# Attention, a two-dimensional Fourier transform and a feed-forward block on one core: transforms folded further along the token axis, three transpose tiles, one set of scheduling preferences

## The chip, the core and the metric

The kernel runs on one core of one Trainium2 chip. The metric is the device time of one launch in microseconds (us), all four batches included. The engines are named as in the profile: PE (TensorE, matrix products), PEld (its weight loads), DVE (VectorE), ACT (ScalarE), POOL (GpSimd) and SP (the engine whose queue issues most of the transfers).

## The reference, cut to what matters

```python
# attention: 4 batches, 8 heads, 1152 keys, 64 features; pairs of queries are averaged -> 576 tokens
q_pool = q.reshape(B, H, S // 2, 2, D).mean(axis=3)
scores = scale * np.matmul(q_pool, k.transpose(0, 1, 3, 2))
attn = np.exp(scores - max) ; attn = attn / sum
attn_out = np.matmul(attn, v)                    # -> x: (4, 576 tokens, 512 channels)
# then per batch
X = np.fft.fft(np.fft.fft(x, axis=1), axis=2)    # over tokens and over channels
u = x + np.real(X)
un = (u - mean) / np.sqrt(var + 1e-06)
out = u + np.maximum(un @ w_ch1, 0.0) @ w_ch2    # 512 -> 2048 -> 512
```

## The kernel before, in words

**Order.** The kernel is written through a recording layer (`Model`). It keeps an estimated clock for every engine and for every operand, and the function `loop` picks at each step what PE gets next by these estimates: a piece of scores (`s_go`), transposes (`t_go`), a piece of weighted values (`a_go`), or a block of the feed-forward part (`block`, "f"). Small background work (loads, normalisations, the transform's elementwise steps) is fed in between by `poll` when an engine is estimated to have room. So the numbers in `_pe`, `_elementwise` and `mood` set the order of the instructions on each engine; the chip then runs each engine's list in order. `mood` draws, for each stretch of 40 us of estimated PE time, a set of preferences from a seed in the list `SEEDS`; `USUAL` is the set without a seed.

**Attention.** 16 pairs of heads, five units each: four units with both heads (128 queries each) and one half unit. A unit is: scores (18 products `s`, three key pieces of 384 columns; a unit of the first kind runs two heads in two row halves of the array), their scaled eviction with running minimum on DVE (`evict`), exp on ACT (`s_exp`), 36 transposes `t` of 64x64 (18 in a half unit) into two PSUM banks at a time, copies of these to SBUF (`pt` for eight key chunks, `ptc` for the ninth) on DVE or ACT, whichever is estimated to end first, and 18 products `o` with the values (`av`). PSUM has seven banks for all of `s`, `t` and `f`, and one for `o`. The tiles `pt` come from a ring of two, or are borrowed from the feed-forward part's rings `g` and `wraw`.

**Transform.** When the four pairs of a batch are done, `dft(b)` computes the real part of the two-dimensional transform. Channels are folded by symmetry into sums and differences (tiles `xs`), tokens too (token t with 576-t), so 289 of 576 token rows are left. The first products go over channels: for three chunks of token rows (97, 96, 96) the folded data are the weights, the tables `cc1` and `cs1` the moving side, split by frequency class (65, 64 and 128 columns for the cosine part, 128 and 128 for the sine part). ACT copies each result to `y`. The second products go over tokens: for two (sine) or three (cosine) column blocks, three products each with 289 moving columns of `cc2` or `cs2` accumulate in one bank; DVE adds the banks to `x` (16 adds over 128 partitions, and two over one). Then `norm(b)` does the layer norm with small products (`lsum`, `sq`, `dg`).

**Feed-forward.** Three fp32r products stand for one (`mm3`). Batches 0 to 2 give 512 of their 576 tokens, 512 columns a product; batch 3 takes the rest with its own, in 384 columns. These products (`f<-unh,w`, `f<-unl,w`, `f<-g,w`) fill gaps in the attention from batch 0's norm on, and are all that is left at the end.

Of the kernel before, what the change touches and what calls it, by code (L numbers as in the profile page):

```python
# [32 lines left out]
TOK = np.concatenate([np.arange(NH), np.arange(SQ - 1, HT, -1)])  # L33
# [12 lines left out]
TCH = [(0, 97), (97, 96), (193, 96)]  # L46
# [178 lines left out]
def _pe(m, op, out, ins, kw):  # L225
# [92 lines left out]
def fused_kernel(ctx: ExitStack, tc: tile.TileContext, k2, q2, v2, w1, w2, cst, out):  # L318
# [26 lines left out]
    cc2 = cp.tile([97, 3, NH], F32, name="cc2")  # L345
    cs2 = cp.tile([97, 3, NH], F32, name="cs2")
# [105 lines left out]
    def s_piece(pr, j, pc, after=None):  # L452
# [8 lines left out]
        for p, k in zip(ps, tiles):  # L461
            if pc == 0:
                sp[k] = spp.tile([P, S], F32, tag="sp", name="sp")
                bia[k] = smp.tile([P, 3], F32, tag="bia", name="bia", bufs=6)
# [25 lines left out]
    HOME = {"pt": (ptp, 2), "g": (gp, 4), "wraw": (cvp, 4)}  # L490
# [101 lines left out]
    def loop(units):  # L592
# [3 lines left out]
        home, where, exps = {}, {}, deque()  # L596
# [11 lines left out]
        def s_cand():  # L608
# [11 lines left out]
            r = [nc.slot("ps_t", "t", 7, len(unit_tiles(pr, j)))]  # L620
# [20 lines left out]
        def t_cand():  # L641
# [4 lines left out]
            if x == 0:  # L646
# [6 lines left out]
                if at["a"][0] < (i if ready and lag[0] or home.get(i - 1) == home[i] else i - 1):  # L653
                    return None
            tiles = unit_tiles(pr, j)
            ks = [tiles[x]] if x < len(tiles) else tiles
            t = nc.slot("ps_t", "t", 7, 2)
            for k in ks:
                if k in exps:
                    t = max(t, max(nc.t["act"], nc.ready(sp[k][:, :])) + 1280 * (exps.index(k) + 1))  # L660
                else:
                    t = max(t, nc.ready(sp[k][:, :]))
            return t

        def t_go():
# [3 lines left out]
            if x == 0:  # L669
                where[i] = {}  # L670
                if j == 0:
                    for x_, (t, r) in enumerate(((cc1, P), (cs1, P), (cc2, 97), (cs2, 97)) if pr == 1 else ()):
# [7 lines left out]
            ks = [tiles[x]] if x < len(tiles) else tiles  # L680
            while any(k in exps for k in ks):
                s_exp(*exps.popleft())
            if x < len(tiles):
# [17 lines left out]
        def a_cand():  # L701
            i, part = at["a"]
            if i == n or i >= at["t"][0]:
                return None
            w = where[i]
            t = 0.0
            for c in range(part * 3, part * 3 + 3):
                for y in range(2):
                    pt, o = w[y, c]
                    t = max(t, nc.ready(pt[:, :, o:o + D]))  # L710
# [55 lines left out]
    def dft(b):  # L766
# [6 lines left out]
        z = tmp[:1, 0, :NH]  # L773
# [18 lines left out]
        bs = mtile([P, NH], F32, "bs")  # L792
# [3 lines left out]

        sets = {0: [], 1: []}
        for y in (1, 0):
            for j in range(2):
                t = xs[y][:, j]  # L800
                yield SB, lambda e: ENG[e].tensor_tensor(t[:, 1:HT], t[:, 1:HT], t[:, NH:], op=(ALU.add, ALU.subtract)[y])
        for y in (1, 0):
            t = xs[y]
            a, c, o = t[:, 0, :NH], t[:, 1, :NH], (xs[1][:, 1, :NH], bs)[y]
            yield SB, lambda e: ENG[e].tensor_tensor(o, a, c, op=ALU.subtract)
            if y:
                yield SB, lambda e: ENG[e].tensor_tensor(a, a, c, op=ALU.add)
                yield CC, lambda e: copy(e, a[:1], c[:1])
                sets[1] += [(a, SSETS[0], slice(0, P)), (o, SSETS[1], slice(P, 2 * P))]
            else:  # L810
                yield SB, lambda e: ENG[e].tensor_tensor(c, a, c, op=ALU.add)
                yield CC, lambda e: copy(e, a, c)
                yield CC, lambda e: copy(e, c[:1], o[:1])
                yield CC, lambda e: copy(e, o[:1], z)
                sets[0] += [(a, CSETS[0], slice(0, 65)), (c, CSETS[1], slice(65, 129)), (o, CSETS[2], slice(129, 257))]

        parts = []
        for y, n in ((1, 256), (0, 257)):
            yy = mtile([97, 3, n], F32, f"y{y}")

            def first(t, t0, m):
                ps = bank()
                c = slice(t0, t0 + m)
# [4 lines left out]
            for t, (t0, m) in enumerate(TCH):  # L828
# [554 lines left out]
```

## Time and profile before

| what | value |
|---|---|
| median of 3 runs | 900.22 us (899.06 to 900.27) |
| the profiled execution | 899.82 us, of which the span of the program's instructions is 898.0 us |
| busy share of the span | PE 98%, PE's weight loads 84%, DVE 66%, ACT 52%, POOL 33% |
| granted TensorE clock, mean | 0.998 of full |

Busy times are from one profiled execution. PE's matmuls are pipelined, so a record's duration holds latency that overlaps its neighbours; what a product costs in a stream is the distance from its start to the start of the next. A product of two fp32 operands shows as two records in the trace and as one in the order of instructions.

### The profile page before, as it was taken

To read this page: it belongs to the slowest core of one execution; us is meant where nothing else is said; L and a number is where in the kernel's file an instruction comes from. 1 tells how busy PE (TensorE), PEld (TensorE's weight loads), DVE (VectorE), ACT (ScalarE), POOL (GpSimd) and SP (SyncE) were. 2 spreads that over 40 slices of the span, in tenths; PEclk is the share of its full clock that TensorE was granted. 3 is DMA by queue.
4 is the path that set the end of the run, shared out by engine and by line. 5 is a ranking of instruction groups with operands and counts; after the bars stand their busy time and mean duration, and the time that the engine had idled before them with its cause. 6 is when DMAs were issued, how large, how long until landed. Compare 5 with 4: busy or idle time off the path is not lost.

```text
span 898.0 us, 22733 instructions
## 1 busy us (share of the span) xinstructions
PE 878.6 (98%) x9044; PEld 755.3 (84%) x9044; DVE 591.0 (66%) x1608; ACT 464.7 (52%) x948; POOL 294.4 (33%) x386
## 2 busy tenths in 40 slices
PE   8999999999999999999998999999999999999998
PEld 6888888788888778878876888888877888999998
DVE  7888889898778978878867756444558323222222
ACT  5777899597667657957743655453522311110110
POOL 2334557655745765367543220300020000000000
PEclk9999999999999999999999999999999999999999
DMA  5553564156868482757570534423393667444432
GB/s 164 176 162 127 174 213 171 49 170 208 285 235 287 144 296 107 266 209 281 160 269 24 202 108 153 147 75 113 90 345 93 184 193 254 148 120 139 118 95 70
DMA packets 54686, 153.28 MB, mean 171 GB/s; under 512 B 15202, under 2 KB 18290, under 8 KB 54580
## 3 DMA queue, kind: packets, MB, share of 16 engines
q1 hardware_dynamic: 49972, 142.07, 47.6%
q0 software_dynamic: 2160, 8.85, 3.2%
q8 instruction: 71, 1.16, 0.5%
q10 hardware_dynamic: 2448, 0.92, 0.4%
q14 instruction: 35, 0.29, 0.1%
HBM read 129.06 MB, written 22.75 MB: 169 GB/s over the span
## 4 chain that ended last, share of the span: by engine, by line
PE 80%; DVE 8%; ACT 5%; issue 4%; DMA 1%; POOL 1%; DVEq 0%; ACTq 0%; POOLq 0%; SPq 0%
PE f L193 47%; PE o L193 14%; PE s L193 13%; PE t L193 7%; DVE sp L193 3%; ACT sp L193 1%; DVE xs L193 1%; ACT pt L193 1%; DVE wa L193 1%; DMA w<-w 1%; DVE pt L193 1%; ACT x L193 1%; DVE x L193 1%; DVE tmp L193 1%; DMA w<-wraw 0%
## 5 line engine op out<-in xcount | busy, mean ns | idle before, releaser
L193 PE MATMUL f<-g,w 128*128 128x512 f32 (+1 forms) x960 | 206.3, 371 | 2.5 <-DMA w<-w 1.3
L193 PEld LDWEIGHTS f<-g,w 128*128 128x128 f32 x960 | 173.2, 188 | 27.8 <-issue 1.9
L193 ACT ACTIVATE sp<-sp,bia 128x1152 f32<-128x1152 f32 x144 | 180.2, 1256 | 27.4 <-DVE sp L193 27.1
L193 PE MATMUL f<-unh,w 128*128 128x512 f32 (+1 forms) x640 | 186.2, 372 | 0.0
L193 DVE TENSOR_SCALAR_CACHE_REDUCE sp<-s,bia 128x384 f32<-128x384 f32 x288 | 162.8, 613 | 6.0 <-PE s L193 2.5
L193 ACT ACTIVATE g<-f 128x512 fp32r<-128x512 f32 (+1 forms) x80 | 44.3, 554 | 222.5 <-PE f L193 222.5
L193 PE MATMUL o<-pt,vs 128*64 128x128 f32 (+1 forms) x2560 | 145.8, 266 | 0.5 <-DVE pt L193 0.4
L193 PEld LDWEIGHTS o<-pt,vs 128*64 128x64 f32 x2560 | 126.9, 137 | 16.9 <-issue 11.7
L193 PEld LDWEIGHTS f<-unh,w 128*128 128x128 f32 x640 | 117.1, 188 | 16.4 <-issue 1.9
L193 DVE SCALAR_TENSOR_TENSOR g<-f,g 128x512 fp32r<-128x512 f32 (+1 forms) x80 | 50.8, 635 | 110.9 <-ACT g L193 110.7
L193 PE MATMUL s<-ksh,qh 64*128 64x384 f32 (+1 forms) x432 | 117.4, 389 | 4.7 <-ACT pt L193 1.1
L193 DVE TENSOR_TENSOR x<-f,x 128x512 f32<-128x512 f32 (+1 forms) x80 | 47.8, 597 | 107.3 <-PE f L193 107.2
L193 PE MATMUL f<-unl,w 128*128 128x512 f32 (+1 forms) x320 | 118.0, 369 | 0.0
L193 PEld LDWEIGHTS t<-ident,sp 64*128 64x128 f32 x2592 | 96.6, 138 | 23.1 <-issue 9.0
L193 PE MATMUL t<-ident,sp 64*128 64x64 f32 x2592 | 110.3, 226 | 4.7 <-DVE sp L193 2.6
L193 ACT COPY pt<-t 128x512 f32<-128x512 f32 x153 | 83.2, 588 | 54.6 <-PE t L193 54.0
L193 DVE COPY pt<-t 128x512 f32<-128x512 f32 x135 | 87.5, 684 | 29.7 <-PE t L193 29.0
L193 PE MATMUL s<-ksh,ql 64*128 64x384 f32 (+1 forms) x432 | 102.9, 350 | 0.1
L193 PE MATMUL s<-ksl,qh 64*128 64x384 f32 (+1 forms) x432 | 98.2, 339 | 0.0
L193 PEld LDWEIGHTS s<-ksh,qh 64*128 64x128 f32 (+1 forms) x432 | 62.7, 189 | 26.0 <-issue 4.4
L193 DVE TENSOR_SCALAR_CACHE_REDUCE sp<-s 128x384 f32<-128x384 f32 x144 | 74.8, 552 | 13.5 <-PE s L193 12.1
L193 POOL TENSOR_TENSOR wa<-wa,wk 128x256 int32<-128x256 int32 x64 | 46.1, 741 | 93.5 <-DVE wa L193 60.9
(100 smaller groups left out, 1038.7 us busy)
## 6 DMA issues: line engine op xcount, KB each, us to landing
w<-w SPq DMA_DIRECT2D x128, 512.0 KB, 3.5
wraw<-in_w SPq DMA_DIRECT2D x32, 512.0 KB, 4.1
w<-wraw SPq DMA_DIRECT2D x32, 512.0 KB, 3.7
qr<-in_q SPq DMA_DIRECT2D x15, 640.0 KB
vs<-in_v SPq DMA_DIRECT2D x16, 576.0 KB, 7.2
ksh<-in_k POOLq DMA_DIRECT2D x15, 576.0 KB, 5.5
kr<-in_k SPq DMA_DIRECT2D x15, 576.0 KB, 6.0
out<-x SPq DMA_DIRECT2D x12, 256.0 KB, 3.4
```

What stands on the lines that cost most here:

```text
L193: return real(*args, **kw)
```

## The change

1. **Transform.** Tokens are folded twice more: the 289 rows are ordered anew (`TOK`), sums and differences of rows t and 288-t are made, and of those with even frequencies once more. The first products then have four chunks of 71 to 76 token rows in place of three of 96 or 97, with the same moving columns. Each second product needs only the frequencies of its class: four products with 73, 72, 144 and 144 moving columns in place of three with 289. Their results are written to every fourth or every second column of the bank. The folds are new elementwise steps on DVE, POOL or ACT, some 14 a batch, between the old ones and the first products.
2. **Transposes.** The ring of `pt` has three tiles. When both heads' exps are near, a group of transposes takes four key chunks of both heads, not eight of one; the weighted values of a unit may start as soon as the chunks of their piece are there.
3. **Estimates and preferences.** The estimated price of fp32 products changes, the seeds are dropped (`SEEDS = []`, so `USUAL` holds throughout), and three new entries (`ws`, `wa`, `both`) tell how much of what follows is asked to be ready.
4. **Small.** The ring `bia` has five tiles (six before), `vt` one (two before). At the end, the second half of each output block of the last batch is sent from ACT's queue, not from SP's.

```diff
-TOK = np.concatenate([np.arange(NH), np.arange(SQ - 1, HT, -1)])
+QT, ET = HT // 2, HT // 4
+TOK = np.concatenate([np.arange(ET + 1), np.arange(QT - 1, ET, -1), [QT]])
+TOK = np.concatenate([TOK, HT - TOK[1:QT], [HT]])
+TOK = np.concatenate([TOK, SQ - TOK[1:HT]])
-TCH = [(0, 97), (97, 96), (193, 96)]
+CCH = [slice(0, 76), slice(71, 147), slice(147, 219), slice(219, 291)]
+SCH = [slice(0, 71), slice(71, 143), slice(143, 215), slice(215, 287)]
+OCH = [slice(0, NH, 4), slice(2, NH, 4), slice(1, NH, 2), slice(1, NH, 2)]
+KCH = [slice(0, 73), slice(73, 145), slice(145, 289), slice(289, 433)]
-        kind, cost = "M", max(n * 4 / 2.4, 112)
+        kind, cost = "M", max(n * 4 / 2.4 + 6, 155)
-    HOME = {"pt": (ptp, 2), "g": (gp, 4), "wraw": (cvp, 4)}
+    HOME = {"pt": (ptp, 3), "g": (gp, 4), "wraw": (cvp, 4)}
...
+            if x < len(tiles) and both[i]:
+                pt = t_tile(512, home[i])
+                spend(t_step(pt, [(k, 4 * x + c) for k in tiles for c in range(4)]))
...
+        a, c = slice(1, QT), slice(QT + 1, HT)
+        yield tt(fs[:, :, 143:286], es[:, :, a], es[:, :, c], ALU.add)
+        for i in (slice(0, 2), slice(2, 3)):
+            yield tt(fc[:, i, 148:291], ec[:, i, a], ec[:, i, c], ALU.subtract)
+        yield tt(es[:, :, a], es[:, :, a], es[:, :, c], ALU.subtract)
+        for i in (slice(0, 2), slice(2, 3)):
+            yield tt(ec[:, i, a], ec[:, i, a], ec[:, i, c], ALU.add)
+        yield tt(fc[:, :, 147:148], ec[:, :, 0:1], ec[:, :, HT:NH], ALU.subtract)
+        a, c = slice(1, ET), slice(ET + 1, QT)
+        yield tt(fs[:, :, :71], es[:, :, a], es[:, :, c], ALU.subtract)
+        yield tt(fs[:, :, 71:142], es[:, :, a], es[:, :, c], ALU.add)
+        yield CC, lambda e: copy(e, fs[:, :, 142:287:QT], es[:, :, ET:QT + 1:ET])
+        yield tt(fc[:, :, :71], ec[:, :, a], ec[:, :, c], ALU.add)
+        yield tt(fc[:, :, 76:147], ec[:, :, a], ec[:, :, c], ALU.subtract)
+        yield CC, lambda e: copy(e, fc[:, :, 71:76], ec[:, :, 0:NH:ET])
...
-                for t, (t0, kk) in enumerate(TCH):
-                    nc.tensor.matmul(ps[:m, :NH], lhsT=yy[:kk, t, j * P:j * P + m], rhs=c2[:kk, t, :],
-                                     start=t == 0, stop=t == 2)
+                for t, (c, o, k) in enumerate(zip(ch, OCH, KCH)):
+                    kk = c.stop - c.start
+                    nc.tensor.matmul(ps[:m, o], lhsT=yy[:kk, t, j * P:j * P + m], rhs=c2[:kk, 0, k],
+                                     start=t < 3, stop=t != 2)
...
-                nc.sync.dma_start(out[b, m, :, c], x[:, c])
+                (nc.scalar if t else nc.sync).dma_start(out[b, m, :, c], x[:, c])
...
-    STEP = 40000
-    SEEDS = [210775, 642599, 0, 377478, 755619, 946008, 803354, 849103, 153896, 905148, 898162, 311019, 110009, 467738, 250890, 919780]
+    STEP = 20000
+    SEEDS = []
```

**First place: PE, the second products of batch 0 and what follows them.** A row is the line, the operation, the tile written and the operands, the shape of the result and how many follow each other; `y` holds the first products' results, `s` are scores. Before:

```order
L193 MATMUL f<-cs_108,y_3190 128x289 x6
L193 MATMUL f<-cc_107,y_3203 128x289 x6
L193 MATMUL f<-cc_107,y_3203 1x289 x3
L193 MATMUL s<-ksh,qh 128x384 x2
L193 MATMUL s<-ksh,ql 128x384 x2
L193 MATMUL s<-ksl,qh 128x384 x2
```

The same place of the changed kernel, from the last full cosine block on:

```order
L199 MATMUL f<-cc_107,y_3439 128x144 x2
L199 MATMUL f<-cc_107,y_3439 1x73
L199 MATMUL f<-cc_107,y_3439 1x72
L199 MATMUL f<-cc_107,y_3439 1x144 x2
L199 MATMUL s<-ksh,qh 128x384 x2
L199 MATMUL s<-ksh,ql 128x384 x2
L199 MATMUL s<-ksl,qh 128x384 x2
L199 MATMUL s<-ksh,qh 128x384 x2
L199 MATMUL s<-ksh,ql 128x384 x2
L199 MATMUL s<-ksl,qh 128x384 x2
L199 MATMUL o<-pt,vs 64x128 x10
L199 MATMUL o<-ptc,vs 64x128 x2
```

Fifteen products with 289 columns became ten of 73 or 72 and ten of 144; behind them stand two pieces of scores and then products `o`, where before three pieces of scores stood.

**Second place: DVE, just ahead of the last batch's second products.** `tmp`, `bs` and `xs` are the folded data, `g` an eviction of the feed-forward part, `x<-x,f` the adds of the second products' banks. Before, from the last pair of token folds on:

```order
L193 TENSOR_TENSOR bs<-xs_10855 128x289
L193 TENSOR_TENSOR xs_10855<-xs_10855 128x289
L193 COPY xs_10855<-xs_10855 1x289
L193 TENSOR_TENSOR xs_10855<-xs_10876 128x289
L193 TENSOR_TENSOR xs_10876<-xs_10876 128x289
L193 TENSOR_TENSOR x<-f,x 128x512
L193 COPY xs_10876<-xs_10876 128x289
L193 COPY xs_10876<-xs_10855 1x289
L193 COPY xs_10855<-tmp 1x289
```

In the changed kernel:

```order
L199 TENSOR_TENSOR tmp<-xs_10901 128x289 x2
L199 TENSOR_TENSOR xs_10889<-bs 128x2x143
L199 SCALAR_TENSOR_TENSOR g<-f,g 128x512
L199 TENSOR_TENSOR xs_10901<-tmp 128x2x143
L199 TENSOR_TENSOR xs_10901<-tmp 128x143
L199 TENSOR_TENSOR bs<-bs 128x2x143
L199 TENSOR_TENSOR tmp<-tmp 128x2x143
L199 TENSOR_TENSOR tmp<-tmp 128x143
L199 TENSOR_TENSOR xs_10901<-tmp 128x3
L199 SCALAR_TENSOR_TENSOR g<-f,g 128x512
L199 TENSOR_TENSOR x<-x,f 128x289
```

Seven folds were added on DVE here (others stand on POOL and ACT), and the copies went to ACT.

**Third place: PE, the half unit of head pair 3 and what stands ahead of it, in the stretch without feed-forward work.** `t<-ident,sp` are transposes, `o` the weighted values, `den` the turned denominators. Before:

```order
L193 MATMUL t<-ident,den 9x64 x2
L193 MATMUL t<-ident,sp 128x64 x16
L193 MATMUL s<-ksh,qh 128x384 x2
L193 MATMUL s<-ksh,ql 128x384 x2
L193 MATMUL s<-ksl,qh 128x384 x2
L193 MATMUL s<-ksh,qh 128x384 x2
L193 MATMUL s<-ksh,ql 128x384 x2
L193 MATMUL s<-ksl,qh 128x384 x2
L193 MATMUL t<-ident,sp 128x64 x20
L193 MATMUL o<-pt,vs 64x64 x16
L193 MATMUL o<-ptc,vs 64x64 x2
```

In the changed kernel:

```order
L199 MATMUL o<-pt,vs 64x128 x16
L199 MATMUL o<-ptc,vs 64x128 x2
L199 MATMUL t<-ident,sp 128x64 x36
L199 MATMUL o<-pt,vs 64x64 x16
L199 MATMUL o<-ptc,vs 64x64 x2
L199 MATMUL s<-ksh,qh 128x384 x2
```

The 36 transposes ahead of the half unit's values, which stood around two pieces of scores, now stand in one run. Over the whole program PE's list has 364 runs of one kind (scores, transposes, values, feed-forward, transform and norm, denominators) before and 371 now.

## Rows read from the trace of the kernel before

**Rows 1.** The page's busy times: us (share of the span) and instructions of each engine.

```profile
PE 878.6 (98%) x9044; PEld 755.3 (84%) x9044; DVE 591.0 (66%) x1608; ACT 464.7 (52%) x948; POOL 294.4 (33%) x386
```

**Rows 2.** The chain that ended last, by engine.

```profile
PE 80%; DVE 8%; ACT 5%; issue 4%; DMA 1%; POOL 1%; DVEq 0%; ACTq 0%; POOLq 0%; SPq 0%
```

**Rows 3.** Busy time in two stages: from, to, length, engines (instructions), clock, DMA.

```profile
0.00:218.00 218.00, 210.09 (x3140) 180.54 (x3142) 189.75 (x596) 170.00 (x343) 111.69 (x152) 0.99 0.47 154
218.00:650.00 432.00, 425.30 (x4639) 352.14 (x4637) 309.37 (x813) 256.47 (x532) 176.19 (x227) 1.00 0.55 185
```

**Rows 4.** What PE waited for longest, whole span: us, times, longest.

```profile
PE t L193 <- DVE sp L193: 2.6, 11, 0.4
```

**Rows 5.** PE's timeline, 395 to 420 us: start, length, instruction, count.

```profile
396.23 1.97 PE L193 MATMUL o<-pt,vs 128*64 128x128 f32 x32
398.03 0.39 PE L193 MATMUL o<-ptc,vs 128*64 128x128 f32 x4
...
400.44 0.50 PE L193 MATMUL s<-ksh,ql 64*128 64x384 f32 x2
400.61 0.51 PE L193 MATMUL s<-ksl,qh 64*128 64x384 f32 x2
...
412.19 0.62 PE L193 MATMUL f<-unh,w 128*128 128x512 f32 x2
...
412.87 0.62 PE L193 MATMUL f<-unh,w 128*128 128x512 f32 x2
...
414.45 1.34 PE L193 MATMUL t<-ident,sp 64*128 64x64 f32 x36
415.60 0.68 PE L193 MATMUL s<-ksh,qh 64*128 64x384 f32 x2
```

**Rows 6.** PE's timeline: the transform of batch 0.

```profile
155.16 0.38 PE L193 MATMUL f<-cs,bs 128*97 128x128 f32 x2
155.37 0.38 PE L193 MATMUL f<-cs,xs 128*96 128x128 f32 x2
156.98 1.92 PE L193 MATMUL f<-cc,xs 128*97 128x65 f32 x18
158.74 3.09 PE L193 MATMUL f<-cs,y 97*128 97x289 f32 x12
161.67 4.65 PE L193 MATMUL f<-cc,y 97*128 97x289 f32 x18
166.25 0.44 PE L193 MATMUL s<-ksh,qh 64*128 64x384 f32 x2
```

**Rows 7.** PE's timeline: products of 96 weight columns and one moving column.

```profile
183.75 1.18 PE L193 MATMUL f<-onesm,sq 128*96 128x1 f32 x12
184.86 0.44 PE L193 MATMUL s<-ksh,qh 64*128 64x384 f32 x2
```

**Rows 8.** DVE's timeline behind the second products of batch 0.

```profile
160.47 5.93 DVE L193 TENSOR_TENSOR x<-x,f 128x289 f32<-128x289 f32 x16 [2.70 <-PE f L193]
166.36 0.81 DVE L193 TENSOR_TENSOR x<-last,f 1x289 f32<-1x289 f32 x2
```

**Rows 9.** DVE's timeline ahead of the last batch's products, and PE's beside it.

```profile
662.37 0.82 DVE L193 TENSOR_TENSOR x<-x,r 128x288 f32<-128x288 f32 x2
676.28 0.30 DVE L193 COPY xs<-tmp 1x289 f32<-1x289 f32 x1
672.88 3.28 PE L193 MATMUL f<-g,w 128*128 128x512 f32 x13 [1.14 <-DVE g L193]
```

**Rows 10.** The end, all engines.

```profile
894.76 0.25 DVE L193 TENSOR_TENSOR rest<-f,rest 128x96 f32<-128x96 f32 x1
895.30 0.39 SPq L193 DMA_DIRECT2D out<-rest  x1
```

**Rows 11.** Busy time while head pairs 1 to 4 are evicted, columns as in rows 3.

```profile
sum 103.90, PE 100.99 PEld 90.22 DVE 90.99 ACT 84.60 POOL 47.11; mean PE 25.25 PEld 22.56 DVE 22.75 ACT 21.15 POOL 11.78
```

**Rows 12.** DVE's copies of eight chunks of transposes, whole span: count | busy us, mean ns.

```profile
L193 DVE COPY pt<-t 128x512 f32<-128x512 f32 x135 | 87.5, 684 | 29.7 <-PE t L193 29.0
```

More of the change, by code (lines that the diff above doesn't have):

```diff
@@ L652, in t_cand, with due @@
                     home[i] = "wraw" if i % 2 and not todo and not busy else "pt"
-                if at["a"][0] < (i if ready and lag[0] or home.get(i - 1) == home[i] else i - 1):
+                if at["a"][0] < (i if ready and lag[0] else i - 1):
                     return None
             tiles = unit_tiles(pr, j)
[L656 to L662, printed above, removed]
+            if x < len(tiles) and x + sum(len(unit_tiles(*units[u])) for u in range(at["a"][0], i) if home[u] == home[i]) >= HOME[home[i]][1]:
+                return None
+            def due(ks):
+                t = 0.0
+                for k in ks:
+                    if k in exps:
+                        t = max(t, max(nc.t["act"], nc.ready(sp[k][:, :])) + 1280 * (exps.index(k) + 1))
+                    else:
+                        t = max(t, nc.ready(sp[k][:, :]))
+                return t
+            t = due(tiles[x:x + 1] if x < len(tiles) else tiles)
+            if x == 0:
+                both[i] = False
+                if j < 4:
+                    t2 = due(tiles)
+                    if t2 <= max(t, nc.t["pe"]) + gait[2]["both"]:
+                        both[i] = True
+                        t = t2
+            t = max(t, nc.slot("ps_t", "t", 7, 2))
             return t
@@ L679, in t_go @@
                         streams.append(head[0])
-            ks = [tiles[x]] if x < len(tiles) else tiles
+            ks = [tiles[x]] if x < len(tiles) and not both[i] else tiles
             while any(k in exps for k in ks):
                 s_exp(*exps.popleft())
-            if x < len(tiles):
+            if x < len(tiles) and both[i]:
+                pt = t_tile(512, home[i])
+                spend(t_step(pt, [(k, 4 * x + c) for k in tiles for c in range(4)]))
+                for c in range(4):
+                    for y in range(2):
+                        where[i][y, 4 * x + c] = pt, (4 * y + c) * D
+            elif x < len(tiles):
                 k = tiles[x]
@@ L702, in a_cand @@
             i, part = at["a"]
-            if i == n or i >= at["t"][0]:
+            if i == n or i not in where or (1, min(part * 3 + 2, 8)) not in where[i]:
                 return None
@@ L706, in a_cand @@
             t = 0.0
-            for c in range(part * 3, part * 3 + 3):
+            for c in range(part * 3, part * 3 + 3 * (1 if nc.mode == "AV" else min(gait[2]["wa"], 3 - part))):
                 for y in range(2):
-                    pt, o = w[y, c]
-                    t = max(t, nc.ready(pt[:, :, o:o + D]))
+                    if (y, c) in w:
+                        pt, o = w[y, c]
+                        t = max(t, nc.ready(pt[:, :, o:o + D]))
             if part == 0:
@@ L800, in dft @@
                 t = xs[y][:, j]
[L801 to L805, printed above, removed]
+                yield tt(t[:, 1:HT], t[:, 1:HT], t[:, NH:], (ALU.add, ALU.subtract)[y])
+        for y, e1, o in ((1, es[:, 0], es[:, 1]), (0, ec[:, 1], ec[:, 2])):
+            a, c = xs[y][:, 0, :NH], xs[y][:, 1, :NH]
+            yield tt(o, a, c, ALU.subtract)
+            yield tt(e1, a, c, ALU.add)
```

85 lines of the change are left out of this document (46 added, 39 removed).

## The prediction

> **What bounds the kernel now.** I first read the page: PE is busy 98% of the span, DVE 66% [rows 1]. A busy share can hold waiting, so next the chain that ended last: 80% of it is PE, 8% DVE, 5% ACT [rows 2]. Then the waits: the longest single pair, PE's transposes waiting for DVE's evictions, is 2.6 us in 898 [rows 4]. So the whole is a PE-bound program, and a us taken from PE's list is a us of the total unless something else then comes late. The stages differ in how near that "something else" is: in the first 218 us DVE is busy 189.75 us (87%), in the mixed stage 309.37 of 432 (72%) [rows 3].
>
> Busy is still not the same as useful. From starts in the timeline [rows 5]: a feed-forward product of 512 columns takes 0.227 us ((412.87 - 412.19)/3), a pair of score products 0.17, a transpose 0.032 ((415.60 - 414.45)/36), a record of the weighted values 0.056 ((398.03 - 396.23)/32). By the program's counts: 1152 x 0.227 + 768 x 0.17 (384 columns, three quarters, my estimate) = 392; scores 1152 x 0.085 + 144 x 0.17 = 122; transposes 2592 x 0.032 = 83; values 2304 x 0.056 + 576 x 0.028 (half the columns) = 145. With 42 for the transforms (next part) that is 784 us. The other 114 us are changes from one kind of run to another, short waits, the start and the norms: over 364 runs at most 0.31 us each.
>
> **Part 1, the products.** Before, in batch 0 [rows 6]: a sine product of the first stage takes 0.21 to 0.22 us (155.16 to 155.37), six of them 1.3; the cosine chunks take 1.76 (156.98 to 158.74, three chunks, 0.587 each); the second stage takes 0.244 us a record ((161.67 - 158.74)/12), 30 records 7.3. Together 10.4 us a batch, 41.6 in all.
>
> After, first stage: eight sine products, 1.75 us (0.45 more). Four cosine chunks: the moving columns alone (257 at 0.22 us for 128) make 0.44 a chunk, the old price 0.587; the weights are narrower (72 to 76 columns against 96 or 97), so I take 0.48, 1.92 in all (0.16 more; bounds 0 and 0.59).
> Second stage: a record of 144 columns at half of 0.244 is 0.122. The 73 and 72 columns would be 0.061 a record by the same scale, but products of 96 weight columns and a single moving one still take 0.09 a record ((184.86 - 183.75)/12, with one change of kind) [rows 7]: weights have a floor, scaled to 128 columns 0.12. A block of 128 columns then costs 4 x 0.12 + 4 x 0.122 = 0.97, the block of one weight column 0.73; per batch 4 x 0.97 + 0.73 = 4.6, saving 2.7 (bounds 2.45 with 0.97 throughout, 3.65 with 0.73).
> Net 2.7 - 0.45 - 0.16 = 2.1 us a batch, **8.4 us in all** (bounds 5.6 and 12.8).
>
> The results of the second stage go to every fourth or second column of a bank. No product of this trace writes so. I price it at nothing, since before's products of 289 columns and of 128 [rows 6] follow their column counts whatever is written; the other end is a doubling of the streams, a rival below. The Trainium skill speaks against this part: "PSUM — Partial Sum Buffer", Specifications, says that a non-contiguous pattern slows matmuls significantly. It gives no figure, and no row here tests it; by it the saving of this part would be gone, without it it stands.
>
> **What the shorter products uncover.** DVE empties their banks with 16 adds in 5.93 us and two more in 0.81, from 160.47, that is 1.73 us behind the first second product; they end at 167.17, 0.9 us behind the products' end at 166.25 [rows 6, 8]. With blocks of 0.97 the first add starts 1.2 us in, all 6.74 end 8.0 us in, the products 4.6 us in: DVE is then 3.4 us behind, 2.5 more than now, and the evictions of the next scores queue behind it. In batch 0 two score pieces (four banks: two never taken, two emptied by then) and 28 products of values, which need no bank of that ring, stand next; the values alone are 28 x 0.11 = 3.1 us and cover it. In batch 1 few transposes and one score piece, then values; in batches 2 and 3 feed-forward products, which need a bank each. I charge 0.25 us a batch, **1.0 us** (0 if covered, 2.5 x 4 = 10 if nothing covers).
>
> **The added folds.** About 14 a batch on DVE, POOL and ACT, 0.30 to 0.45 us each on DVE by the like ones (two of 288 columns in 0.82, a one-row copy 0.30 [rows 9]). None is PE's, so they cost only where the products wait for them. In batches 0 to 2 attention or feed-forward work stands ahead, and the order puts the products where `Model` believes the folds done. In the last batch I compared lists: between the norm's `dg` products of batch 2 and the first transform products PE has 96 feed-forward products, 21.8 us, and the two `dg`, 1.0. Before, it had 120 and the end of attention. DVE's list for that stretch, priced by before's rows of the same kind, is some 24 us (its part from 662.37 to 676.58 alone is 14.2 [rows 9]), with about 3 us of new folds in it, and POOL's last sine folds follow DVE's. Already before PE waited 1.14 us for DVE there [rows 9]. I add **1.5 us** (0 to 4).
>
> **Part 2 and 3, the order.** Every transpose, score and value product stays. The orders have 364 runs before, 371 now: 7 x 0.31 = **2.2 us** more. By kind, changes from scores to values rise from 27 to 42 and from scores to feed-forward fall from 23 to 16, so I keep 0 and 5 as bounds. The ring of three lets a unit's first tile of transposes run ahead of the former unit's values, and values start on part of a unit: it takes away waits of the kind in rows 4, which are too small to pay more than 2 to 3 us.
> Copies move: the orders have 248 copies of transposes on DVE where 213 were, ACT 200 for 235. While pairs 1 to 4 are evicted, eight-chunk copies on DVE rise from 30 to 41, at 0.684 us [rows 12] 7.5 us. That stretch took 103.90 us with DVE busy 90.99 [rows 11], so DVE would go from 88% to 95%. I take it as covered, since PE's own list is as long as before; if not, it is a rival. The rings `bia` (five for at most four live score tiles) and `vt` cost nothing for that reason.
>
> **Part 4.** SP issues the last `rest` at 895.30, 0.29 us behind the end of DVE's add at 895.01 (894.76 + 0.25), since the block's second half is issued ahead of it [rows 10]; from ACT's queue that is free: **0.3 us** less. The transfer's landing is no shorter.
>
> **Sum.** -8.4 + 1.0 + 1.5 + 2.2 - 0.3 = -4.0 us, on the profiled execution's own 899.82 us (span 898.0, 1.8 around it) 895.8; the runs' median is 0.4 us above that execution, so **896 us**.
>
> **The rivals.**
> *Strided results stream at half speed (slower).* Second stage 5 blocks x 2 x 0.73 = 7.3 us, as long as before; the first stage is 0.61 longer; part 1 turns from -8.4 to +2.4. Total -4.0 + 10.8: **907 us**. It decides from a factor near 1.5: blocks of 1.1 us eat the 4.0 us. For it: no row excludes it, since none writes so. Against: only that nothing in the trace grows with what is written, which is weak. 15%. (The page named under part 1, "PSUM — Partial Sum Buffer" of the Trainium skill, is the rule that would bring it.)
> *DVE or lost preferences eat it (no change).* If PE waits for the 7.5 us of copies in pairs 1 to 4, less a third that DVE's idle 12.9 us there absorbs, +5 us: **901 us**. The same size follows if without seeds the 114 us of changes and waits grow by a twentieth. For it: 87% DVE [rows 3]; against: 2.6 us of waits [rows 4]. 22%.
> *Fewer waits and no weight floor.* Part 1 at 12.8, and the third tile pays its 3 us: **889 us**. 13%.
>
> **How the numbers follow.** The forecast's own case has 50%, with 891 to 900 by its bounds. Runs of before spread by 1.2 us, so 0.2% (1.8 us) is about what can be told from no change. Faster than 898.4: 0.43 of the forecast, 0.13 of the third, 0.04 of the second: 0.60. Slower than 902.0: 0.12 of the first, 0.08 of the second: 0.20. The range takes 888 to 906: the third rival's and most of the first's.
>
> **What the new profile would show.** Second-stage records: 30 of 0.244 us become 20 of about 0.12 and 20 of 0.06 to 0.12 a batch; records of 0.24 at 144 columns would mean half speed. The first add of DVE behind the transform some 1.2 us behind the first second product, and evictions 3 us behind the last. PE idle for ACT or DVE `xs` ahead of the last transform: up to 2 us. DVE's copies 0.684 each, 145 in place of 135, and DVE's share of the first 218 us at 90% or above with the pairs' stretch still near 104 us; a stretch of 109 would show the second rival. Wrong would be: pairs far quicker or slower than 26 us each, so that the order and not the products sets the change.

## The result: 8.5 us slower, where 4 us faster was forecast

The changed kernel takes 908.67 us (median of five runs, 907.81 to 909.83) against 900.22 before; the ratio is 1.0094, 95% interval 1.0080 to 1.0109. The profiled execution took 909.83 us with a span of 908.0, 10.0 longer than before's span. Its mean granted TensorE clock is 0.992, before's 0.998. One of the ten executions of tuned_fold below, of 1184.37 us at a granted clock of 0.649, is left out of its median.

The page after, busy times and the chain that ended last:

```profile
PE 878.8 (97%) x9124; PEld 758.5 (84%) x9124; DVE 607.0 (67%) x1666; ACT 461.4 (51%) x934; POOL 306.3 (34%) x402
...
PE 73%; DVE 14%; issue 6%; ACT 4%; POOL 1%; DMA 1%; SPq 0%; DVEq 0%; ACTq 0%; POOLq 0%
```

PE's busy time is that of [rows 1], although its products are cheaper now: more of it is work at half speed (below). The chain tells more: DVE's share rose from 8% to 14% [rows 2]. Next the windows by stage (columns as in [rows 3]), and pairs 1 to 4 as the last line:

```profile
0.00:138.00 138.00, 133.12 (x2012) 113.57 (x2013) 123.24 (x387) 100.60 (x204) 63.54 (x89) 0.98 0.52 178
138.00:251.00 113.00, 103.98 (x1466) 88.95 (x1466) 100.34 (x283) 84.99 (x172) 70.08 (x92) 0.98 0.44 143
251.00:640.00 389.00, 379.84 (x4278) 316.37 (x4278) 278.33 (x776) 232.71 (x475) 160.73 (x208) 1.00 0.54 183
640.00:908.00 268.00, 261.84 (x1376) 239.61 (x1374) 105.09 (x222) 43.12 (x85) 11.97 (x14) 1.00 0.49 154
...
sum 105.30, PE 103.14 PEld 90.44 DVE 99.01 ACT 82.00 POOL 51.26; mean PE 103.14 PEld 90.44 DVE 99.01 ACT 82.00 POOL 51.26
```

From 138 to 251 us PE is idle for 9 us of 113. In before it is idle for 2.6 in the same window:

```profile
138.00:251.00 113.00, 110.41 (x1381) 92.54 (x1378) 97.04 (x270) 85.26 (x173) 72.53 (x95) 1.00 0.54 180
```

The pairs' stretch is only 1.4 us longer than in [rows 11], with DVE at 94%.

PE's waits (us, times, longest):

```profile
PE t L199 <- DVE sp L199: 5.4, 12, 2.8
PE o L199 <- ACT x L199: 3.7, 4, 1.6
PE o L199 <- ACT pt L199: 1.6, 2, 1.0
...
PE f L199 <- POOL xs L199: 1.2, 1, 1.2
```

The pair of [rows 4] has doubled, and its longest wait went from 0.4 to 2.8 us. Waiting for ACT's copy out of the one `ps_o` bank is new. The list's rows of 0.5 us and more add up to 22.3 us; before's to 12.6.

PE's timeline: a first stage (batch 0), a second stage (batch 2), and the longest wait with what followed it:

```profile
155.77 0.75 PE L199 MATMUL t<-ident,sp 64*128 64x64 f32 x16 [2.79 <-DVE sp L199]
...
157.57 3.42 PE L199 MATMUL o<-pt,vs 128*64 128x128 f32 x32
...
171.23 1.97 PE L199 MATMUL f<-cs,xs 128*71 128x128 f32 x16
173.04 2.10 PE L199 MATMUL f<-cc,xs 128*76 128x65 f32 x24
174.98 2.04 PE L199 MATMUL f<-cs,y 71*128 71x73 f32 x16
...
511.28 2.04 PE L199 MATMUL f<-cs,y 71*128 71x73 f32 x16
513.16 2.88 PE L199 MATMUL f<-cc,y 76*128 76x73 f32 x24
515.97 0.73 PE L199 MATMUL f<-unh,w 128*128 128x512 f32 x2
```

A sine stage takes 1.81 us (171.23 to 173.04), the cosine chunks 1.94, the second stage 4.69 (511.28 to 515.97): 8.44 a batch. Read in the same way, from start to start, [rows 6] has 1.3, 1.76 and 7.51 (158.74 to 166.25), 10.57 a batch; that saves 2.13 a batch and 8.5 us in all. So the products came out as forecast (8.4), and some 18.5 us were lost elsewhere in this execution.

The 32 products of values behind the wait took 3.42 us instead of the 1.97 of [rows 5]. The window over them says why; its clock column is 0.50, that is 1.2 GHz, after a PE that had been idle for 2.79 us:

```profile
157.20:160.60 3.40, 3.40 (x37) 3.28 (x35) 2.79 (x11) 3.35 (x6) 1.21 (x2) 0.50 0.53 173
```

What POOL did ahead of that wait, by its timeline:

```profile
150.13 1.58 POOL L199 TENSOR_TENSOR xs<-x 128x288 f32<-128x288 f32 x2
151.66 1.42 POOL L199 TENSOR_TENSOR wraw<-wa,wraw 128x256 fp32r<-128x256 f32 x2
153.04 1.52 POOL L199 TENSOR_TENSOR xs<-xs 128x287 f32<-128x287 f32 x2
```

And DVE beside it, with its adds behind the products of batch 0 as the last line:

```profile
150.64 4.24 DVE L199 TENSOR_TENSOR xs<-x 128x288 f32<-128x288 f32 x1
...
155.17 0.54 DVE L199 TENSOR_SCALAR_CACHE_REDUCE sp<-s 128x384 f32<-128x384 f32 x1
...
176.12 5.92 DVE L199 TENSOR_TENSOR x<-x,f 128x289 f32<-128x289 f32 x16 [3.03 <-PE f L199]
```

One DVE add of 128x288, of which two take 0.82 us in [rows 9], lasted 4.24, until POOL had ended six two-input operations that it ran without a gap. The evictions behind it came late, and PE waited for them.

An account of the profiled execution: the mean clock c puts 2(1 - c) of the span at half speed. That is 14.5 us after and 3.6 before, so up to 5.5 us more work time (some of the time at half speed may be waiting). Listed waits are 9.7 longer, products 8.5 shorter: +6.7 of the span's +10.0. I put the other 3.3 down to the seven more runs on PE and to waits under 0.5 us, without having shown it.

### The profile page after: what moved, and what is told of

It is laid out like the page before. It is cut to its first block, busy times and chain, and to the rows that moved or that the text cites. A ratio compares the mean times of both kernels' runs of the same rounds, so it can differ in the third digit from the quotient of the medians.

```text
span 908.0 us, 22959 instructions
## 1 busy us (share of the span) xinstructions
PE 878.8 (97%) x9124; PEld 758.5 (84%) x9124; DVE 607.0 (67%) x1666; ACT 461.4 (51%) x934; POOL 306.3 (34%) x402
## 4 chain that ended last, share of the span: by engine, by line
PE 73%; DVE 14%; issue 6%; ACT 4%; POOL 1%; DMA 1%; SPq 0%; DVEq 0%; ACTq 0%; POOLq 0%
PE f L199 44%; PE o L199 13%; PE s L199 11%; PE t L199 7%; DVE sp L199 5%; DVE pt L199 2%; ACT sp L199 2%; DVE x L199 1%; DVE xs L199 1%; DVE wa L199 1%; DVE d L199 1%; DVE unl L199 1%; ACT pt L199 1%; DMA w<-w 0%; DMA wraw<-in_w 0%
## 5 line engine op out<-in xcount | busy, mean ns | idle before, releaser
L199 PE MATMUL o<-pt,vs 128*64 128x128 f32 (+1 forms) x2560 | 149.5, 269 | 6.1 <-ACT x L199 3.7
L199 PEld LDWEIGHTS o<-pt,vs 128*64 128x64 f32 x2560 | 129.6, 139 | 22.8 <-issue 11.5
L199 PEld LDWEIGHTS f<-unh,w 128*128 128x128 f32 x640 | 116.8, 188 | 18.6 <-DVE sp L199 1.8
L199 PE MATMUL s<-ksh,qh 64*128 64x384 f32 (+1 forms) x432 | 113.5, 394 | 5.3 <-DVE pt L199 1.5
L199 DVE COPY pt<-t 128x512 f32<-128x512 f32 x145 | 93.5, 683 | 21.6 <-PE t L199 19.7
L199 ACT COPY pt<-t 128x512 f32<-128x512 f32 x143 | 77.7, 590 | 40.3 <-PE t L199 39.6
L199 PE MATMUL s<-ksh,ql 64*128 64x384 f32 (+1 forms) x432 | 98.0, 349 | 0.1
L199 PE MATMUL s<-ksl,qh 64*128 64x384 f32 (+1 forms) x432 | 94.2, 339 | 0.0
L199 PEld LDWEIGHTS s<-ksh,qh 64*128 64x128 f32 (+1 forms) x432 | 58.8, 189 | 28.4 <-DVE pt L199 6.0
```

The costliest lines, as they stand in the source:

```text
L199: return real(*args, **kw)
```

## The experiments

Theories at the start. A: the rules of the new order are the loss. B: the load of the added folds (for products_only: a PE that runs ahead only waits for DVE). D: any plan made anew loses, since the seeds belong to one plan. "Order unchanged" means that every other instruction of every engine stands where it stood. Times are medians; the last column is 2(1 - c) of the profiled span, the time at half clock to about 1 us (before: 3.6). It differs between executions of one kernel: 7.3 to 14.5 in after's five, 0 to 12.6 in later ones of before, but for one of 902.80 us whose clock of 0.947 doesn't fit this account. So only large differences in it say something.

| kernel | us | ratio to before (95%) | half clock, us |
|---|---|---|---|
| after | 908.67 | 1.0080 to 1.0109 | 14.5 |
| products_only | 898.91 | 0.9968 to 0.9994 | 3.6 |
| fold_only | 928.64 | 1.0275 to 1.0358 | 27.7 |
| before_plain | 928.29 | 1.0287 to 1.0331 | 24.1 |
| ghost | 905.44 | 1.0037 to 1.0075 | 7.2 |
| after_long | 917.57 | 1.0181 to 1.0231 | 7.3 |
| fold_plain | 922.23 | 1.0235 to 1.0274 | 23.9 |
| hold_off | 907.93 | 1.0074 to 1.0106 | 7.2 |
| tuned_after | 907.41 | 1.0059 to 1.0103 | 21.7 |
| tuned_fold | 905.10 | 1.0028 to 1.0061 | 10.8 |
| ring2 | 908.30 | 1.0068 to 1.0131 | 10.9 |
| no_chunks | 916.85 | 1.0168 to 1.0198 | 16.5 |
| fold_frozen | 926.84 | 1.0253 to 1.0308 | 23.9 |
| no_early | 916.35 | 1.0134 to 1.0210 | 27.5 |
| nudge_f | 908.79 | 1.0072 to 1.0113 | 14.5 |
| nudge_turn | 915.22 | 1.0140 to 1.0180 | 23.9 |
| one_set | 905.79 | 1.0044 to 1.0078 | 7.2 |
| fold_frozen_dve | 924.64 | 1.0236 to 1.0287 | 31.4 |

**products_only.** Before's order, short second-stage products alone.

```diff
-nc.tensor.matmul(ps[:m, :NH], lhsT=yy[:kk, t, ...], rhs=c2[:kk, t, :], start=t == 0, stop=t == 2)
+GHOST.matmul(...)   # Model counts the old product, the engine gets none
+for t, (o, w) in enumerate(((slice(0, NH, 4), 73), (slice(2, NH, 4), 72), (slice(1, NH, 2), 144), (slice(1, NH, 2), 144))):
+    tc.nc.tensor.matmul(ps[:m, o], lhsT=yy[:72, t % 3, ...], rhs=c2[:72, t % 3, :w], start=t < 3, stop=t != 2)
```

> The kernel before, every engine's order unchanged; only the 30 second-stage products of a batch are replaced by the 40 shorter ones with strided results (their weights are cut to 72 rows, no folds are added, so the transform's values are left out). Theory A (the products are worth what the forecast said, the loss is in the new order): 4 x 2.7 = 10.9 us less on PE, 1 us given back where DVE's adds fall behind, so about 890 us. Theory B (a PE that runs ahead in the transform only waits for DVE, so the saving is not to be had): 898 to 901 us.

898.91 us: 1.3 gained of the 10.9 forecast, which is 11.3 by the starts (7.51 us a batch before, 4.69 after). The ten executions lie between 895.5 and 901.2; PE's timeline of the profiled one, of 896.80, shows where the lead went, and the last line is before's:

```profile
163.42 0.45 PE L193 MATMUL s<-ksh,qh 64*128 64x384 f32 x2
...
166.02 0.41 PE L193 MATMUL s<-ksh,qh 64*128 64x384 f32 x1 [1.05 <-DVE x L193]
...
174.73 1.53 PE L193 MATMUL o<-pt,vs 128*64 128x128 f32 x24
...
174.79 1.42 PE L193 MATMUL o<-pt,vs 128*64 128x128 f32 x22
```

The scores behind the transform start at 163.42 where they started at 166.25 [rows 6], 2.8 us ahead. A new wait for a bank that DVE's adds hold takes 1.05, and at 174.73 the values stand where those of before stood at 174.79: within 12 us the lead is gone. That is theory B's number, and its reason here: in an order that was fitted to the longer products, DVE is what ends last here.

**after_long.** The reverse in the order of after: the products put back to 289 columns.

```diff
+for t in range(3):
+    tc.nc.tensor.matmul(ps[:m, :NH], lhsT=yy[:71, t, ...], rhs=c2[:71, 0, :NH], start=t == 0, stop=t == 2)
```

> The kernel after, every engine's order unchanged, with the second-stage products put back to 30 of 289 contiguous columns a batch (weights of 71 rows, so the transform's values are left out). The reverse of the run that shortened them in the order of before. If the shorter products are worth what the forecast said where the order was planned for them: 908.7 + 4 x 2.7 = 919 us. If PE would wait for DVE and ACT behind a transform anyhow, as it did in the order of before (2.7 us shorter a batch, about 0.5 gained): 909 to 912 us.

917.57, 8.9 us more than after. Where the plan was made for them, 8.9 of the shorter products' 11.3 us arrive. So the same products are worth 1.3 or 8.9, by the order that they stand in.

**ghost.** The order of after without the new folds.

```diff
-yield tt(fs[:, :, 143:286], es[:, :, a], es[:, :, c], ALU.add)
+yield gt(fs[:, :, 143:286], es[:, :, a], es[:, :, c], ALU.add)   # counted by Model, not issued
...
```

> The kernel after, every engine's order unchanged, with the batch's 14 new folds left out on the engines (Model still counts them; the transform's values are then wrong in the parts that the folds make). Theory B (folds' load): most of the 18 us lost come back, 891 to 897 us. Theory A or D (order): the folds are off the path but for the waits before a transform, so 904 to 909 us.

905.44: the folds cost 3.2 us in the order of after. In this order it is not theory B.

**before_plain**, **fold_only**, **fold_plain.** Three corners between before and after.

```diff
-    SEEDS = [210775, 642599, 0, 377478, ...]
+    SEEDS = []
```

> The kernel before with its sixteen seeds taken out, so that one set of preferences holds throughout; nothing else. If the seeds are what was lost (theory D): 908 to 918 us, since the change then loses some 17 us by them or by what comes with them. If ring, gates and folds are what was lost: 899 to 903 us.

> The kernel before with the transform's change alone: folds, shorter products, their tables and Model's price of such a product; seeds, ring of two and the old rules of transposes and values stay, though the order is planned anew round the shorter transform. Theory A (the order's rules are the loss): 900.2 - 8.4 + about 3 = 893 to 896 us. Theory B (the added folds on DVE and POOL are the loss): 905 us or more, as after. Theory D (any plan made anew loses, since the sixteen seeds belong to one plan): 903 to 910 us, with the loss spread over the attention stages and not only behind the transforms.

> The kernel before with the new transform and without the seeds: ring of two, whole units, and one set of preferences. Against the kernel after it differs by the ring of three, the transposes by key chunks and the early values alone. If these bring what the seeds gave up (before without seeds took 928.3): 922 to 930 us, so that parts 2 and 3 without the seeds gain 14 to 20. If they are worth little and the new transform is what helped: 908 to 914 us.

928.29, 928.64 and 922.23. One path from before to after reads: seeds out +28.1, new transform (with its new price) -6.1, ring and rules (with part 4) -13.6, together +8.45. Another reads: new transform +28.4, seeds out -6.4, ring and rules -13.6. So the 28 us belong neither to the seeds nor to the transform alone; they are lost as soon as seeds and operations don't fit each other. Of the theories D fits best, though it expected 908 to 918 and 903 to 910 us, 10 to 19 us less than came. A fails, since the new rules gain. With the new transform the old seeds don't help at all (928.64 with them, 922.23 without). What a plan without them looks like, in before_plain, by the timelines of POOL, DVE and PE in turn, and then a window:

```profile
155.71 3.04 POOL L193 TENSOR_TENSOR ksl<-kr,ksh 128x288 fp32r<-128x288 f32 x4
158.71 2.40 POOL L193 TENSOR_TENSOR ql<-qr,qh 128x320 fp32r<-128x320 f32 x2
```

```profile
154.92 4.11 DVE L193 TENSOR_SCALAR wa<-wa 128x512 f32<-128x512 f32 x1
```

```profile
161.05 0.69 PE L193 MATMUL s<-ksh,qh 64*128 64x384 f32 x1 [4.87 <-DVE pt L193]
...
164.22 3.25 PE L193 MATMUL o<-pt,vs 128*64 128x128 f32 x32
```

```profile
160.10:166.90 6.80, 5.85 (x43) 5.42 (x45) 5.80 (x17) 0.00 (x0) 1.93 (x3) 0.50 0.00 0
```

The same three steps as in after: a DVE operation (0.55 us by its mean in before) lasts 4.11 while POOL runs without a gap, PE waits 4.87 for the copies behind it, and then works at 1.2 GHz. In before no DVE operation from SBUF to SBUF takes longer than this one:

```profile
170.29 2.14 DVE L193 TENSOR_SCALAR wa<-wa 128x512 f32<-128x512 f32 x1
```

Before's granted clock is 0.91 in the first 20 us and 1.00 over the rest. Of before_plain's 28 us some 10 are clock (20.5 us more at half speed) and 18.6 listed waits (31.2 us in rows of 0.5 us and more, before 12.6).

**ring2**, **no_chunks**, **no_early.** Parts 2 and 3, one rule at a time taken out of after.

```diff
-HOME = {"pt": (ptp, 3), ...}                      # ring2
+HOME = {"pt": (ptp, 2), ...}
-"both": 800.0                                     # no_chunks
+"both": -1e9
-if i == n or i not in where or (1, min(part * 3 + 2, 8)) not in where[i]:   # no_early
+if i == n or i >= at["t"][0]:
```

> The kernel after with the ring of two tiles in place of three (the rule that counts the tiles in use goes by two); chunk rules and early values stay, no seeds. If the third tile is what gained most of the 13.5 us: 916 to 922 us. If the chunk rules and early values did: 907 to 911 us.

> The kernel after with the ring of three and the early values, but transposes never taken by chunks of both tiles (the preference that allows it is set so that it never holds). If taking chunks of both tiles is what gained: 915 to 922 us. If the third tile did: 907 to 911 us. Both near 915 would say that each is half of it.

> The kernel after with the old rule for values: a unit's values are offered only when all its transposes stand, not on part of them; ring, chunks and the single set of preferences stay. What is left of the 13.5 us of parts 2 and 3 beside the chunks (8.2) and the ring (0) is 5.3: if it is the early values', 913 to 915 us; if it is only what any new plan may differ by, 904 to 912.

908.30, 916.85 and 916.35: the third tile is worth nothing, chunks 8.2 us, early values 7.7, which is above both of its ranges; its four executions lie between 911.8 and 918.7. The next two runs say how little a single such difference proves.

**nudge_f**, **nudge_turn.** One preference of after, shifted a little.

```diff
-"f": 300.0, "turn": 100.0
+"f": 320.0, "turn": 100.0     # nudge_f
+"f": 300.0, "turn": 110.0     # nudge_turn
```

> The kernel after with one of its preferences nudged: a feed-forward product is offered 320 ns later by the planner's account instead of 300. No rule, no instruction and no price changes, only which of two near candidates comes first. If a plan's time follows its rules: 907 to 910.5 us. If it is in good part chance, which candidate happened to be first: 3 us or more away from 908.7 on either side.

> The kernel after with another preference nudged: the charge for a change of kind on PE 110 ns instead of 100. As for the other nudge: 907 to 910.5 us if the rules set the time, 3 us or more away on either side if chance has a good part in it.

908.79 and 915.22. A charge of 110 ns in place of 100 costs 6.5 us. Its profiled execution, at 921.67 the slowest of five, has one more long wait:

```profile
342.48 0.64 PE L199 MATMUL s<-ksh,qh 64*128 64x384 f32 x2 [3.99 <-DVE x L199]
```

The other four have 16 to 20 us at half clock by their mean clocks. So plans under the same rules can differ by some 6 us. What both rules gained together (13.6) is twice that; how much each did can't be told.

**tuned_after**, **tuned_fold**, **one_set.** Preferences picked anew for the new plans.

```diff
-    SEEDS = []
+    SEEDS = [913297, 54373, 647943, ...]     # tuned_after, STEP = 40000; tuned_fold: others, on fold_plain
-"f": 300.0, "turn": 100.0, "tv": 1.15, "wa": 1, ...
+"f": 150, "turn": 0, "tv": 1.3, "wa": 2, ...   # one_set
```

> The kernel after with sixteen sets of preferences of its own (SEEDS of 40 us each, picked one window at a time by the end that the planner reckons for its plan). The runs so far: taking the old seeds away costs 28.1 us, the new transform gains 6.1 without seeds (928.3 to 922.2), ring and chunk rules gain 13.5 (922.2 to 908.7). If rules and seeds take away the same waits, the total comes out by the transform alone: 900.2 - 6 = 892 to 897 us. If they take away different waits and add up: 908.7 - 28 = 880 to 886 us. If seeds picked by the planner do nothing on the chip: 904 to 912 us.

> The kernel before with the new transform, ring of two and whole units, and sixteen sets of preferences picked for that plan in the same way (with the old seeds it took 928.6, with none 922.2). If seeds belong to the plan that they were picked for and are worth as much here as in the kernel before: 922.2 - 28 = 894 us, 891 to 899, which is the new transform's own worth, 6 us under before. If the old seeds were worth 28 us by something that picking for the planner's end does not give: 905 to 920 us.

> The kernel after with another single set of preferences throughout, picked by the end that the planner reckons for its plan. If seeds were worth their 28 us because preferences must vary over time: 905 to 912 us, as after. If they were worth it because one plan out of many was picked, one set picked out of many gives most of it too: 893 to 901 us. Idle PE followed by half clock, which the planner reckons only roughly, can spoil the pick: then 905 us or more with several stretches at half clock.

907.41, 905.10 and 905.79. For fold_plain the pick gives 17 of the 28 us, for after 1.3, and one picked set throughout 2.9. Neither adding up (880 to 886) nor 894 came true, and no version that computes the whole beats before. tuned_after has 21.7 us at half clock (its other executions 11 to 25), which the planner reckons only roughly: what it picks as short isn't short on the chip. The kernel's text shows one thing that the planner leaves out: `Model.run` lets a DVE operation wait for no more than the one POOL operation that runs when it would start, and `_elementwise` lets one whose output has 16 elements a partition or fewer wait for none. So the holds of 4 us and more in these traces are not in its account. How before's sixteen were picked can't be seen here, so why they do better stays open.

**fold_frozen**, **fold_frozen_dve.** The complete new transform in before's order.

```diff
+def swap(engs, old, new, more=(), move=False):
+    def fn(e):
+        put(GHOST, e, *old)
+        if nc.probing is None:
+            put(RAW, "dve" if move and e == "pool" else e, *new)
+            for x, *y in more:
+                put(RAW, x, *y)
+    return engs, fn
```

`old` is what Model counts, `new` what the engine does, `more` the added folds; `move` is set in fold_frozen_dve alone, for four folds of batch 0.

> The new transform, complete, put into the order of the kernel before: seeds, ring and rules as before, and the planner still counts the old folds and products, so that every other instruction of every engine stands where it stood; the 13 added folds a batch are issued right behind the old ones (ten on DVE, one on POOL, two on ACT), and the fourth first-stage chunk takes a bank more. It is what the forecast's sum without its order term meant: -8.4 + 1.0 + 1.5 = -5.9, so 894 us. By the runs so far: the shorter products alone gained 1.3 there (898.9), leaving out the folds gained 3.3 in the order of after, so about 902 us, no gain. If DVE's added folds stand ahead of evictions that PE waits for: 904 to 908 us.

926.84, far beyond every expectation: 26.6 us lost. The first wait, by the timelines of POOL, DVE and PE:

```profile
145.55 3.07 POOL L200 TENSOR_TENSOR xs<-xs 128x287 f32<-128x287 f32 x4
148.59 1.56 POOL L457 TENSOR_TENSOR bs<-xs 128x289 f32<-128x289 f32 x2
150.11 1.53 POOL L457 TENSOR_TENSOR tmp<-xs 128x289 f32<-128x289 f32 x2
151.62 1.66 POOL L200 TENSOR_TENSOR qr<-qr 128x320 f32<-128x320 f32 x2
```

```profile
147.69 5.61 DVE L459 COPY bs<-xs 1x2 f32<-1x2 f32 x1
```

```profile
154.16 2.13 PE L200 MATMUL t<-ident,sp 64*128 64x64 f32 x32 [4.34 <-DVE sp L200]
```

A copy of two elements took 5.61 us. In before the same copy took 1.45: there POOL stopped at 149.51 to wait for DVE, and 0.16 us were enough; the new folds need no such wait, and POOL runs on. Before's POOL and DVE there:

```profile
148.71 0.80 POOL L193 TENSOR_TENSOR bs<-xs 128x289 f32<-128x289 f32 x1
149.67 0.85 POOL L193 TENSOR_TENSOR xs<-xs 128x289 f32<-128x289 f32 x1 [0.16 <-DVE tmp L193]
...
148.07 1.45 DVE L193 COPY tmp<-xs 1x2 f32<-1x2 f32 x1
```

If that is the cause, less for POOL and more for DVE should help:

> The run with the new transform in the old order, with one thing changed in batch 0: the four 128x289 adds and subtracts that POOL issues behind its four 128x287 (POOL ran ten two-input operations without a gap there, from 145.55 to 153.28, while a DVE copy of two elements took 5.61 us and PE waited 4.34 us for the evictions behind it) are issued by DVE. If the hold by POOL's unbroken run is the cost: the copy ends when POOL's 128x287 end, below 1.5 us, the wait of 4.34 falls below 1.5 us, less time at half clock, and 926.8 falls by 4 to 8, to 919 to 923 us, though DVE has 1.8 us more to do. If DVE's load is the cost: 1.8 us and more on top, 927 to 931 us.

```profile
148.31 2.33 DVE L459 COPY bs<-xs 1x2 f32<-1x2 f32 x1
```

```profile
152.24 0.81 PE L200 MATMUL t<-ident,sp 64*128 64x64 f32 x16 [1.99 <-DVE sp L200]
```

The copy fell to 2.33 and the wait to 1.99, both above the 1.5 expected; the total fell by 2.2 to 924.64, less than the 4 to 8, and less than the runs of either kernel spread (920.5 to 928.8). The hold is confirmed by the rows, the total leaves its price open. With the shorter products alone before's order took 898.91: in it the added folds and the fourth chunk cost 27.9 us, where the folds cost 3.2 in the order of after. So a plan kept to the letter loses as much as one made anew, and theory B, refuted for after's order, is true of before's.

**hold_off.** The 4.24 us hold of after taken away: its add and the one behind it go to POOL.

```diff
+onpool = Engine(nc, tc.nc.gpsimd, "dve")       # Model counts DVE, POOL does it
+if b == 0 and len(seen) == 3: return onpool    # the third add that DVE was given
```

> The kernel after, every PE, ACT and SP order unchanged; in batch 0 alone the one 128x288 add that DVE held for 4.24 us while POOL ran six two-input operations back to back, and the one-row add behind it, are issued by POOL instead, at their places. If the hold cost what its rows show (PE's 2.79 us wait at 155.77, and 3.4 us at half clock behind it, which doubles 32 products of values from 1.97 to 3.42): 908.7 - 2.5 - 1.5 = 904 to 905.5 us. If the time is lost again at the next wait, as PE's lead was in the run with shorter products: 907 to 909 us.

907.93, 0.7 gained. PE's timeline:

```profile
151.97 1.97 PE L199 MATMUL o<-pt,vs 128*64 128x128 f32 x32
...
157.56 0.44 PE L199 MATMUL s<-ksh,qh 64*128 64x384 f32 x1 [1.86 <-DVE ptc L199]
...
159.88 3.43 PE L199 MATMUL o<-pt,vs 128*64 128x128 f32 x30
```

The first values run at full speed at 151.97, 5.6 us earlier than in after; then PE waits 1.86 for DVE, whose next two folds took 1.86 beside a running POOL, where they took 0.83 in after, and the next values are at half clock:

```profile
154.41 1.86 DVE L199 TENSOR_TENSOR bs<-xs 128x289 f32<-128x289 f32 x2
```

The time was lost again at the next wait, as the rival had it. I read from it that this stretch is bound by the work on DVE and POOL together and not by one hold; no run shows that alone.

In the profiled executions every kernel above 912 us has a DVE operation of 4.1 to 6.3 us beside POOL, except fold_frozen_dve, whose longest takes 2.80. But after, ring2, ghost and nudge_f have one of 4.2 to 4.3 too, and tuned_after one of 5.2. So such holds go with the loss, and their share of it stays open.

## Why the prediction was wrong

**The products** were right: 0.94 us a block of 128 columns (0.97 forecast), 3.75 for the first stage (3.67), 8.5 us saved for 8.4. One reading was low: the second stage's 18 cosine records take 0.254 us in [rows 6] ((166.25 - 161.67)/18), not the sine records' 0.244, so the stage took 7.5 us before and not 7.3. The rival of strided results gave 907 us, nearly the time that came, by a mechanism that did not occur: 144 columns written to every second place take 0.12 us, half of the 0.244 of [rows 6]. The rule of the Trainium skill ("PSUM — Partial Sum Buffer", Specifications), that non-contiguous patterns slow matmuls significantly, does not show for these results; the measurement decides.

**What they uncover** was put at 1.0: 2.4 in the order of after (11.3 - 8.9). In the order of before it would have been 10.0 (11.3 - 1.3), the bound of 10 that the text gave "if nothing covers". DVE's first add did start 1.1 us behind the first second product, and the adds ended 3 us behind the last, as forecast.

**The added folds** at 1.5: 3.2 by the ghost run, inside their bounds (0 to 4), but in the order of after alone. The wait for POOL ahead of the last batch's products is 1.22 us.

**The last `rest`** is issued 0.03 us behind its add (0.29 before): the 0.3 us are there.

**The order, "7 x 0.31 = 2.2 us", is the step that failed.** -8.5 + 2.4 + 3.2 - 0.3 is -3.2, so with +8.5 measured some +11.7 are left for it, as far as parts that were measured one at a time add up. It counted runs on PE and priced them at before's mean excess. But that mean was a property of before's seeded plan: taking the seeds out costs 28.1 us by itself, with about as many runs (352 among the records of its trace, 365 among before's). What an order costs, as I read the traces, is whether evictions and copies stand in DVE's list where PE needs them; run counts don't show it. The claim that waits of [rows 4] are "too small to pay more than 2 to 3 us" took the small waits for a property of the program. They were the outcome of the plan, and without the seeds ring and rules paid 13.6.

**The second rival** named the right cause, lost preferences, and gave it 5 us of a cause that has 28, half won back by the chunk and value rules. Its test was wrong too: pairs 1 to 4 stayed at 105.3 with DVE at 94%, so the 7.5 us of copies were covered, as the forecast held. The forecast's own sign of being wrong, pairs far from 26 us each, did not show either (26.3), although it was the order that set the change. Of the 9.8 us that PE is idle more, 6.4 lie from 138 to 251 us, where the first transform's folds meet the evictions. **Not in the sum at all** was the clock: a PE that works at 1.2 GHz behind a wait pays for the wait again. Apart from after_long, the profiled executions of kernels above 912 us have 16 to 31 us at half clock; those below have 4 to 15, but for tuned_after.

## What to carry to other kernels

When a schedule was picked for one program, a change to the program can lose what the pick had won, whether the order is planned anew (28.4 us here) or kept (26.6). Price that first, by the plan with its preferences taken out, before pricing the operations. A saving on the bounding engine arrives only if the next engine's list has room where it falls: the same products were worth 1.3 us in one order and 8.9 in another. A difference of a few us between two such plans says nothing about a rule until a nudge that changes no rule has shown how far plans scatter (6.5 us here).

## What the hardware showed that was not expected

A DVE operation from SBUF to SBUF can be held by a run of POOL operations: 4.24 us for a 128x288 add (0.41 in [rows 9]) and 5.61 for a copy of two elements (0.16 at 158.27 in after), both until POOL's run ended, and 4.11 for a 128x512 tensor_scalar (mean 0.55 in before), behind which POOL ran on. The evictions from PSUM behind them took their usual 0.54 to 0.62 beside a running POOL. The Trainium skill ("SBUF — State Buffer", "SBUF: two separate sides") says that of a GpSimd operation and a DVE operation in a two-port mode, or one with two inputs in SBUF beside a GpSimd operation that reads SBUF, the one that starts first gets a shared port pair for the whole instruction and the other fully blocks. These rows agree on the block (no row shows the mode of the copy and the tensor_scalar), but here it lasted through six to eight POOL instructions in a row, not one. It is not always so: in before a 128x288 add at 142.34 took 1.13 us, while POOL's four adds ran from 141.59 to 145.09. What decides between the two is not shown.

Behind waits of 1.86 to 4.87 us PE's products soon ran at 1.2 GHz, 32 products of values in 3.25 to 3.42 us instead of 1.97. Not every such wait did it: behind one of 2.03 us at 686.27 in products_only and one of 2.12 at 698.26 in fold_frozen the clock column is 1.00.
